# Six weight loads cut into a transfer of 40 rows and one of 24 rows, in a kernel of sparse attention followed by a spectral mix

## The chip, the cores and the metric

The kernel runs on one core of one Trainium2 chip. The metric is the time of one execution on the device in microseconds (us), as the median of several runs. All inputs lie in the chip's memory as 32-bit floats; the kernel turns them into 16-bit floats while it loads them.

## The reference

The first half is causal attention with 8 batches, 8 heads, 576 positions and 64 columns per head. Heads 0 to 3 see the last 32 positions, heads 4 to 7 see every 32nd position. The second half takes the result as x (8 x 576 x 512), goes to frequencies, mixes the lowest 64 of them with a complex 512 x 512 matrix each, comes back, and ends in a channel product:

```
X = np.fft.rfft(x, axis=1)
Xr, Xi = real and imaginary part of X[:, :64]
Yr = einsum('bmd,mde->bme', Xr, w_r) - einsum('bmd,mde->bme', Xi, w_i)
Yi = einsum('bmd,mde->bme', Xr, w_i) + einsum('bmd,mde->bme', Xi, w_r)
y = np.fft.irfft(Y, n=576, axis=1)        # Y is zero above mode 63
u = x + y
out = u + max(u @ w_ch, 0)
```

The weights w_r and w_i are 64 matrices each of 512 x 512. They are 134 MB as 32-bit floats, and each is used once.

## The kernel before

The weights are a stream of 128 tiles. Tile i holds, for mode m = i % 64, one half of the 512 input rows (the upper half for i < 64, the lower for i >= 64): 256 rows of w_r in partitions 0 to 63 and the same 256 rows of w_i in partitions 64 to 127, four rows to a partition. The function `w_fetch` makes the next tile and issues its loads on GpSimd's queue: one transfer for w_r and one for w_i, each of 64 partitions by 2048 numbers, which is 256 KB as it lands and twice that as it is read (line 190). Mode 0 has no imaginary part, so tiles 0 and 64 have one transfer. That makes 254 transfers. In what follows a "row" is one partition's 2048 numbers, so a transfer has 64 rows.

The tiles live in a pool of 11 buffers (`NWBUF`), besides six early "guests" in other buffers. Each transfer issued from GpSimd takes one of eight completion semaphores in turn, and the issue waits until the transfer that used that semaphore eight places earlier has landed. A tile's first transfer also waits for TensorE to be done with the buffer. GpSimd's queue carries the loads of q, k and v as well: pieces of 64 rows (line 216), small pieces of 8 rows (line 222) and pieces of 128 shorter rows (line 234).

The work has four stages. The strided heads come first, with loads ahead of them. Then the local heads run, and the first 64 calls of `mode` (slot 0) are spread between their steps. The third stage runs `mode(1, m)` for the other 64 tiles, between the transposes and channel products of `turn` and `premix` (lines 587 to 651). Each `mode` is 16 products of a weight block with the spectra X (line 543) and, at its end, one call of `w_fetch`, so one tile is ordered for one used. The order of the steps on TensorE is the order in which they are written. The fourth stage comes after the last mode: it turns the spectra back, adds, and writes the output, with no weights left to load.

Tiles are numbered by `i`, so the tile used by `mode(slot, m)` is i = 64 * slot + m.

Of the kernel before, what the change touches and what calls it, by code (L numbers as in the profile page):

```python
# [19 lines left out]
NM = 64  # L20
# [59 lines left out]
def kernel(  # L80
# [10 lines left out]
    nc = tc.nc  # L91
# [76 lines left out]

    GUEST = {3: ("Y0", 0), 4: ("Y0", 1), 5: ("X0", 0), 6: ("X0", 1)}
    GUEST |= {15: ("YT", 0), 16: ("YT", 1)}  # L170
    guests = {}
    w_tiles = []
    w_chs = {}

    def w_fetch(n=1):
        for _ in range(n):
            i = len(w_tiles)
            if i >= 2 * NM:
                return
            half, m = 1 - i // NM, i % NM  # L180
            if i in GUEST:
                n, j = GUEST[i]
                if j == 0:
                    guests[n] = big.tile([128, 2, 4, DM], F16, tag=n, name="wt")
                wt = guests[n][:, j]
            else:
                wt = pw.tile([128, 4, DM], F16, tag="w", name="wt")

            for ri, src in enumerate([moe_w_r, moe_w_i] if m else [moe_w_r]):
                nc.gpsimd.dma_start(  # L190
                    wt[ds(64 * ri, 64)],
                    src[m, ds(256 * half, 256), :].rearrange("(p c) e -> p c e", c=4),
                )
            w_tiles.append(wt)

    def w_ch_fetch():
# [335 lines left out]
    def mode(slot, m):  # L532
# [17 lines left out]
        if slot or m not in GUEST:  # L550
            w_fetch()
# [145 lines left out]
    const_load(nc.sync, "cMl", "cFl", "cA")  # L697
    load_str(2)
    w_fetch(2)

    def str_front(b):
# [39 lines left out]
    for b in range(B):  # L741
        if b < 5:
            load_str(b + 3)
        load_loc(*[(), (), (), (), (0,), (1, 2), (3,), (4, 5)][b])
        w_fetch([3, 3, 2, 2, 2, 1, 1, 1][b])
        front = str_front(b + 1) if b + 1 < B else loc_front(0)
        for t in range(6):
            str_scores(b, t)
            if b > 0:
                if t < 2:  # L750
                    str_values(b - 1, 4 + t)
                elif t == 2:
                    dft(b - 1, 1)
            if t >= 2:
                str_values(b, t - 2)
            for w in front[SPLIT[t] : SPLIT[t + 1]]:
                w()
        if b == 1:
            nc.vector.memset(PL[:, 0:PS0], 0.0)
# [241 lines left out]
```

The softmax here doesn't subtract the row's maximum and nothing guards it: scores larger than these inputs give would overflow.

## Time and profile before

| | |
|---|---|
| median of 6 runs | 438.34 us (437.3 to 439.75) |
| profiled execution | 437.52 us, span from first to last instruction 435.7 us |
| busy share of the span | TensorE 77%, VectorE 50%, ScalarE 43%, GpSimd 43% |
| mean granted TensorE clock | 0.838 of full speed |
| bytes moved | 92.20 MB as it lands, 163.22 MB read from memory |
| GpSimd's transfer queue | 26800 packets, 81.29 MB, 94.8% of the 16 transfer engines' time |
| one weight transfer | 256 KB, 9.4 to 9.6 us from issue to landing (median) |

The profile follows one execution. A transfer is done by 16 transfer engines side by side; a full row of 2048 numbers is one packet of 4096 bytes as it lands, and an engine works on one packet after the other. The chain of waits goes back from the last instruction to whatever released it, again and again, and so shows what set the time in each stretch. The profiled execution took 1.82 us more than its span, for what lies before the first and after the last instruction.

### The profile page before, as it was taken

The numbers are of one execution on the slowest core, as the hardware profiler recorded it, in microseconds if no ns is written. First come the engines' busy times: TensorE is split into PE (matmuls) and PEld (weight loads), VectorE is DVE, ScalarE is ACT, GpSimd is POOL, SyncE is SP. The second block draws the span as 40 slices with busy tenths as digits, with TensorE's granted clock in tenths as the row PEclk, the third lists the DMA queues.
The fourth block names the chain that finished last, engine by engine and source line by source line (L and its number), as shares of the span: only waits on it lengthen the run. The fifth ranks groups of instructions, "written<-read, shape, count | busy, mean of one in ns | idle before, by whom it ended". The sixth has DMA issues, their size and how long they took to land.

```text
span 435.7 us, 12328 instructions
## 1 busy us (share of the span) xinstructions
PE 334.8 (77%) x5289; PEld 241.4 (55%) x5289; DVE 215.9 (50%) x466; ACT 188.4 (43%) x353; POOL 186.7 (43%) x339
## 2 busy tenths in 40 slices
PE   1988778779897878787775566778685858988994
PEld 1866667558776666576653344445444545554441
DVE  2786887935335243343411033344344443764895
ACT  1585777744554345434441201123222312443882
POOL 6545353333444343444343444344344344420883
PEclk9996999979888678967865559686978688999999
DMA  8999999999999999999999999999999999991687
GB/s 172 207 211 211 211 212 212 211 209 212 213 210 213 211 208 211 212 212 212 212 209 214 211 211 212 212 212 213 199 212 212 212 211 213 211 211 36 266 323 281
DMA packets 31094, 92.20 MB, mean 212 GB/s; under 512 B 6144, under 2 KB 7168, under 8 KB 31040
## 3 DMA queue, kind: packets, MB, share of 16 engines
q0 software_dynamic: 26800, 81.29, 94.8%
q1 hardware_dynamic: 3440, 9.46, 5.8%
q8 instruction: 42, 0.69, 0.6%
q10 hardware_dynamic: 800, 0.67, 0.6%
q14 instruction: 12, 0.10, 0.1%
HBM read 163.22 MB, written 9.44 MB: 396 GB/s over the span
## 4 chain that ended last, share of the span: by engine, by line
DMA 75%; PE 15%; issue 4%; DVE 3%; ACT 1%; POOL 1%; DVEq 0%; POOLq 0%
DMA wt<-in_moe_w_i_dram 56%; DMA wt<-in_moe_w_r_dram 11%; DMA ring<-in_q_dram 6%; PE sc L641 2%; DMA ring<-in_v_dram 2%; PE u L684 2%; PE v L684 2%; PE v L886 2%; PE y L543 1%; DVE yy L674 1%; PE u L905 1%; PE tp L281 1%; PE tp L320 1%; PE tp L649 1%; DVE xT L593 1%
## 5 line engine op out<-in xcount | busy, mean ns | idle before, releaser
L543 PE MATMUL y<-X,wt 128*128 128x16 f16 (+1 forms) x2048 | 82.6, 192 | 60.7 <-DMA wt<-in_moe_w_i_dram 58.4
L190 POOL DMA_DIRECT2D wt<-in_moe_w_r_dram x128 | 65.8, 514 | 120.0 <-DMA wt<-in_moe_w_r_dram 34.2
L543 PEld LDWEIGHTS <-wt 128*128 128x128 f16 (+1 forms) x2048 | 72.2, 103 | 75.1 <-issue 54.1
L190 POOL DMA_DIRECT2D wt<-in_moe_w_i_dram x126 | 64.8, 514 | 67.1 <-DMA wt<-in_moe_w_i_dram 49.3
L650 ACT ACTIVATE v<-sc 128x512 f16<-128x512 f32 x32 | 19.0, 597 | 86.0 <-PE sc L641 85.9
L641 PE MATMUL sc<-w_cp,xT 128*128 128x512 f16 (+1 forms) x160 | 49.1, 434 | 0.5 <-DVE xT L613 0.4
L467 ACT ACTIVATE PL<-sc 128x480 f16<-128x480 f32 (+1 forms) x48 | 27.7, 579 | 46.2 <-PE sc L453 45.7
L651 DVE COPY xo<-tp 128x512 f16<-128x512 f16 x32 | 22.1, 692 | 41.9 <-PE tp L649 41.9
L246 DVE TENSOR_TENSOR xb<-av,rec 90x256 f16<-90x256 f32 (+2 forms) x80 | 36.0, 450 | 2.8
L245 DVE RECIPROCAL rec<-av 90x4 f32<-90x4 f32 (+2 forms) x80 | 14.7, 183 | 42.8 <-PE av L482 30.4
L398 DVE COPY qT<-tp 128x576 f16<-128x576 f16 x16 | 12.0, 758 | 41.2 <-PE tp L391 38.3
L256 ACT ACTIVATE v<-tp 128x640 f16<-128x640 f16 (+1 forms) x24 | 19.4, 807 | 20.3 <-PE tp L425 16.7
L391 PE MATMUL tp<-cI_s,ring 64*64 64x64 f16 x864 | 26.4, 212 | 1.9 <-DVE kz L398 1.2
L356 ACT ACTIVATE PL<-sc 90x360 f16<-90x360 f32 (+1 forms) x48 | 22.9, 490 | 10.7 <-PE sc L349 10.0
L899 POOL TENSOR_TENSOR rl<-rl,xo 128x512 f32<-128x512 f32 x16 | 18.3, 1156 | 18.2 <-ACT rl L897 17.9
L916 DVE TENSOR_TENSOR osb<-u,rl 128x512 f32<-128x512 f32 x36 | 23.6, 689 | 2.6 <-PE u L684 1.5
L391 PEld LDWEIGHTS <-ring 64*64 64x64 f16 x864 | 21.0, 124 | 6.6 <-issue 3.6
L437 PE MATMUL sc<-cMl_s,cI_s 128*128 128x480 f16 (+1 forms) x48 | 22.6, 471 | 1.6 <-ACT X L256 1.6
L453 PE MATMUL sc<-qT,kz 128*128 128x160 f16 (+1 forms) x160 | 22.6, 267 | 1.3 <-issue 1.3
L281 PE MATMUL tp<-cI_s,ring 72*128 72x72 f16 x256 | 15.2, 207 | 10.4 <-DMA ring<-in_v_dram 7.8
L453 PEld LDWEIGHTS <-kz 128*128 128x128 f16 x160 | 16.3, 117 | 11.6 <-issue 8.9
L897 ACT ACTIVATE rl<-v 128x512 f32<-128x512 f32 x36 | 20.4, 597 | 4.2 <-PE v L684 3.5
(98 smaller groups left out, 641.0 us busy)
## 6 DMA issues: line engine op xcount, KB each, us to landing
wt<-in_moe_w_r_dram POOLq DMA_DIRECT2D x128, 256.0 KB, 9.4
wt<-in_moe_w_i_dram POOLq DMA_DIRECT2D x126, 256.0 KB, 9.6
out_dram<-osb SPq DMA_DIRECT2D x14, 512.0 KB, 2.7
ring<-in_v_dram POOLq DMA_DIRECT2D x8, 288.0 KB, 10.2
ring<-in_q_dram POOLq DMA_DIRECT2D x8, 288.0 KB, 10.6
ring<-in_k_dram POOLq DMA_DIRECT2D x8, 288.0 KB, 10.6
ring<-in_v_dram POOLq DMA_DIRECT2D x8, 256.0 KB, 8.5
ring<-in_q_dram POOLq DMA_DIRECT2D x8, 256.0 KB, 8.4
```

What stands on the lines that cost most here:

```text
L190: nc.gpsimd.dma_start(wt[ds(64 * ri, 64)], src[m, ds(256 * half, 256), :].rearrange("(p c) e -> p c e", c=4),)
L246: nc.vector.tensor_tensor(out=dst, in0=val.rearrange("p h (q c) -> p h c q", c=4), in1=rec[0:n, 0:pieces] .to_broadcast((n, pieces, 64)) . ...
L356: nc.scalar.activation(out=PS[0:n, ds(POFF[t], 4 * n)], in_=scp[0:n, 0 : 4 * n], func=ACTF.Exp, scale=SCALE,)
L391: nc.tensor.transpose(tp[ds(64 * hp, 64), ds(64 * i, 64)], qn[ds(64 * hp, 64), ds(64 * (9 * g + i), 64)], idn[ds(64 * hp, 64), ds(64 * hp, ...
L437: nc.tensor.matmul(scp[:, 0 : n * times].rearrange("p (h x) -> p h x", h=times), idn, mask_rows("cMl", n, times), start=True, stop=False,)
L453: nc.tensor.matmul(scp[:, ds(col, n)], kzs[par][:, hp, ds(s0, 128)], qTs[par][:, ds(s0, n)], start=False, stop=(i == len(todo) - 1),)
L467: nc.scalar.activation(out=dst, in_=src, func=ACTF.Exp, scale=SCALE)
L543: nc.tensor.matmul(yv[:, mi, e, :], wt[pr, XC[c], ds(128 * e, 128)], Xh[half][pr, c, :, :, m], start=(c == 0), stop=(c == 3),)
L641: nc.tensor.matmul(vp[pr, :], xT[:, ch, cols], w_chs["cp"][:, ch, :], start=(ch == 0), stop=(ch == 3),)
L651: nc.vector.tensor_copy(out=xo[pr].rearrange("p (h q c) -> p h q c", h=2, c=4), in_=tp[pr, 0:512].rearrange("p (h c q) -> p h q c", h=2, c=4),
L897: nc.scalar.activation(out=rl, in_=vp, func=ACTF.Relu)
L916: nc.vector.tensor_tensor(out=osb[:, t % 2, :], in0=up, in1=rls[b, t][:, t % 2, :], op=AluOp.add)
```

## The change

In six of the 128 tiles (i = 28, 45, 62, 79, 96 and 113) the load of the w_r part is issued as two transfers, one of the first 40 rows and one of the remaining 24, in place of one of 64 rows. The same bytes go to the same places. The w_i parts and the other tiles are loaded as before.

```
     GUEST |= {15: ("YT", 0), 16: ("YT", 1)}
+    CUT = range(28, 2 * NM, 17)
...
             for ri, src in enumerate([moe_w_r, moe_w_i] if m else [moe_w_r]):
-                nc.gpsimd.dma_start(
-                    wt[ds(64 * ri, 64)],
-                    src[m, ds(256 * half, 256), :].rearrange("(p c) e -> p c e", c=4),
-                )
+                rows = src[m, ds(256 * half, 256), :].rearrange("(p c) e -> p c e", c=4)
+                cuts = (0, 40, 64) if i in CUT and not ri else (0, 64)
+                for a, z in zip(cuts, cuts[1:]):
+                    nc.gpsimd.dma_start(wt[64 * ri + a : 64 * ri + z], rows[a:z])
             w_tiles.append(wt)
```

GpSimd's queue has 336 rows of program in place of 330; the other engines have the same number of instructions in the same order. The first product of a cut tile waits for three semaphores in place of two, and the transfers behind a cut use the next semaphore in the circle of eight.

## The prediction

> **What bounds the kernel now.** I read the page's strip of slices first, then the chain of waits, then who waits for the weights.
>
> ```profile
> PE   1988778779897878787775566778685858988994
> DMA  8999999999999999999999999999999999991687
> ...
> q0 software_dynamic: 26800, 81.29, 94.8%
> ...
> L543 PE MATMUL y<-X,wt 128*128 128x16 f16 (+1 forms) x2048 | 82.6, 192 | 60.7 <-DMA wt<-in_moe_w_i_dram 58.4
> ```
>
> The transfer engines are full from the first slices to slice 36 (about 392 us), and TensorE's idle time before the mode products is put down to the w_i transfer, 58.4 of 60.7 us. So the stream of weights sets the pace. The chain says how evenly:
>
> ```profile
> 317.41 9.63 DMA wt<-in_moe_w_i_dram
> 327.04 0.28 issue
> 327.32 9.63 DMA wt<-in_moe_w_i_dram
> 336.95 0.28 issue
> 337.23 9.63 DMA wt<-in_moe_w_i_dram
> ...
> 366.82 0.65 PE y L543 x16
> ```
>
> Each link is a transfer, then the issue of the transfer eight places behind it, which had to wait for its semaphore. So eight transfers take 9.63 + 0.28 = 9.91 us, one takes 1.239 us. With 64 rows on 16 engines, an engine does four packets in that time: about 0.305 us each and 0.02 us for its completion mark.
>
> A transfer has landed when its slowest engine has. The trace holds 16 landing marks for each transfer; no view prints them, so I give them in numbers. For the weight transfer that lands at 137 us the first and the last mark are 3.0 us apart, for one at 253 us 4.3 us, for the last weight transfer (396.56 us) 4.2 us. Then eight engines lie within 0.4 us of the first, and the other eight between 3.4 and 4.2 us behind it. The cause stands in the queue list:
>
> ```profile
> q8 instruction: 42, 0.69, 0.6%
> ```
>
> These are 42 blocks of program of 16 KB, 0.9 to 1.3 us each. Their durations recur in a cycle of eight (893, 893, 948, 945, 936, 974, 974, 962 ns), and at each one landing mark steps back by about 1.07 us. So eight engines take turns at them, about five each by the end, and the stream runs at the pace of these eight. None of the 16 stands idle: each shows 1.239 us for every weight transfer.
>
> Last, how the stream hands over to the end. In the stretch from 340 to 400 us TensorE waited for weights only this long, and the last tile is used 1.0 us after it landed:
>
> ```profile
> PE y L543 <- DMA wt<-in_moe_w_i_dram: 5.6, 5, 1.5
> ```
> ```profile
> 395.73 0.64 PE L543 MATMUL y<-X,wt 128*128 128x16 f16 x16
> 397.08 1.12 PE L543 MATMUL y<-X,wt 128*128 128x16 f16 x32 [0.72 <-DVE YT L571]
> ```
>
> Setting each tile's landing against its use: tiles 109 to 115 are used 0.05 to 0.3 us after they land, tiles 116 to 119 0.25 to 0.7 us after, tile 125 4.2 us after. So from about 367 us the chain is TensorE's and VectorE's own work, started by tile 115. A delay of the stream before that reaches the end less about 0.25 us of slack (tile 118); a gain reaches it only as far as TensorE can follow.
>
> **The change part by part.** *Issues.* Six transfers more on GpSimd's queue. The form with 8 rows, the nearest to a small one, takes 0.57 us to issue, the 64-row form 0.51 us:
>
> ```profile
> L222 POOL DMA_DIRECT2D ring<-in_q_dram x4: 573/573/591, 3.0 to 51.9; - x4
> ```
> ```profile
> L190 POOL DMA_DIRECT2D wt<-in_moe_w_r_dram x128: 509/515/554, 14.4 to 385.9; - x128
> ```
>
> Six times 0.57 us is 3.4 us, beside a queue that stands waiting for landings (97 us in all). Behind the added issue on that queue are the tile's w_i load and the following tiles; they wait for a landing anyway. Price: nothing. Without that cover it would be up to 3.4 us.
>
> *Semaphores.* Two small transfers hold two of the eight places, so the queue holds up to one transfer (1.24 us) less. From issue to the first landing mark a late weight transfer takes 5.0 to 5.4 us, against 4.1 us for the kernel's very first transfer, which found the engines empty. So about 1 us of work lies queued before the leading engine, and some 5 us before a lagging one. With 1.24 us less, a leader may stand idle for a moment at a cut, a laggard never does, and only the laggards set the pace. Price: nothing; without that cover up to 0.3 us a cut, 1.5 us in all.
>
> *Completion marks.* What an engine without data pays shows in the 8-row pieces of line 222. Their packets go to eight engines only, two each (0.63 us), and the other eight spend 0.04 us on marks. One more transfer is thus 0.02 to 0.04 us per cut and engine: 0.12 to 0.24 us for six, on every engine. I take 0.24.
>
> *The split of the rows.* This is the term that decides. 64 rows are four for each of 16 engines; 40 and 24 rows are not multiples of 16, so some engines get more than four of the tile's rows and some fewer. No weight transfer before shows how. The nearest row is the 8-row piece: twelve of them, one set of eight engines and the other in turn. Three bounds follow.
> - Same engines each time: five rows in place of four on most engines, laggards among them, six times: 6 x 0.305 = +1.83 us. With the marks, +2.07 us.
> - Shares move on from cut to cut: what is left over is at most about one piece, 0.63 - 0.04 = 0.59 us, on a few engines. With the marks, +0.24 to +0.83 us.
> - All eight laggards are spared a row each time: -1.83 + 0.24 = -1.59 us, and the leaders, at 0.4 + 2.07 = 2.5 us, stay ahead of the laggards' 4.2 - 1.6 = 2.6 us.
>
> Would dealing 40 rows to one set of eight (five each) and 24 to the other (three each) spare the laggards? I followed the marks through the pieces between 27 and 62 us. The engines that never fetch program come from both sets, so laggards sit in both, and the set with five rows would hold some: again +1.83 us. I therefore take the first bound as the likeliest.
>
> A rule that bears on this stands in the Trainium skill, DMA: Bandwidth & Descriptors, section on why a DMA increments its semaphore by 16: the number of engines is the largest one up to 16 that divides the row count, and fewer than 16 start where the last such transfer ended. By it, 40 rows are ten engines with four and 24 rows twelve with two; over six cuts four engines end two rows up, four two rows down, and the estimate from that page is between -0.4 and +0.8 us. The same section reports an exception for transfers from GpSimd: all 16, with the rounded-up share each. By that, 40 rows are three each and 24 two each, so the first twelve engines do five rows each time, an estimate of +1.9 us. The alternating 8-row pieces agree with the rule's start that moves on; no run here shows which of the two holds for 40 rows. The page's rules for kernel authors also advise against two transfers to disjoint partition halves, since the parts share the same engines.
>
> *Sum.* The stream's slowest engine is 2.07 us later by tile 113; less 0.25 us of slack is 1.8 us. The last laggards differ by 0.8 us among themselves, so the worst need not be hit fully: I take 1.7 us. The profiled 437.52 us become 439.2. That execution lies 0.82 us under the median, so on the scale of medians: 438.34 + 1.7 = 440.0 us. What this kernel's measurement can tell from no change is about 0.3%, or 1.3 us.
>
> **The rivals.** *The shares even out* (0.29). For it: the 8-row pieces do move on. Against it: a start that moves is seen only for transfers on half the engines. +0.24 to +0.83 us in the stream, less 0.25: 0 to 0.6 us, so 438.3 to 438.9 us. No change that can be told.
>
> *The laggards are spared* (0.15), the other side. If the rows dealt less fall on the eight engines that fetch the program, the slowest engine gains up to 1.59 us. For it: six cuts of one row either way are 3.7 us between two sets of eight, and the gap to close is 3.4 to 4.2 us. Against it: both sets of the 8-row pieces hold laggards. TensorE must follow: in the slack table tile 105 is used 4.1 us after it lands, and it has caught up by 109, so it can follow most of it. About -1.3 us: 437.0 us. It decides from about three rows of relief on each of the eight; with fewer the worst of them stays.
>
> *The cut does nothing because the loads are the same bytes* would be the first rival with no marks: 438.3 us; it is in its chance.
>
> **How the numbers follow.** Uneven shares on fixed engines has 0.56, and its own range is 439.3 (the worst laggards hit in part, +1.0) to 440.9 us (+2.07, no slack, and half a us of scatter; the runs before spread from 437.3 to 439.75). The range for 8 in 10 takes in the first rival and goes from 437.9 to 441.0 us. Of the forecast some falls under 0.3%, of the first rival some above, and these are about equal: faster 0.15, same 0.29, slower 0.56.
>
> **What would show it.** Right: in the chain, links of 9.63 us as before except around the six cuts, where a link grows by about 0.3 us; the last weight transfer lands about 2 us later than 396.56; the 16 marks of the late transfers lie further apart than 4.2 us; TensorE's wait for weights grows. The even rival would show the same last landing within 0.8 us, the other one a last landing near 395 us and marks closer together. Wrong altogether would be a stream in which engines stand idle at the cuts (a queue run dry), or a chain that no longer goes through the weights before 366 us.

## The result and the profile after

The change costs time: 440.80 us as the median (439.77 to 442.31), against 438.59 us for the kernel before beside it. The ratio is 1.0051, with a 95% interval from 1.0040 to 1.0061, so +2.2 us (1.8 to 2.7). All changes of the time in us below are worked out from such ratios; the medians alone give up to 0.6 us more or less. The profiled execution took 440.23 us with a span of 438.3 us; before they were 437.52 and 435.7 us. The forecast was 440.0 us, about 1.7 us slower; of the 0.8 us between it and 440.80 us, 0.25 us is the median of the kernel before, which was 438.34 us when the forecast was made. All lines of the kernel after stand three or more higher: the weight load is L196, the mode products L546.

The strips and the two rows of the page that answer to those of before:

```profile
PE   1977787779795988878854567678585859988994
DMA  8999999999999999999999999999999999991687
...
q0 software_dynamic: 26992, 81.29, 94.8%
...
L546 PE MATMUL y<-X,wt 128*128 128x16 f16 (+1 forms) x2048 | 82.1, 192 | 62.3 <-DMA wt<-in_moe_w_i_dram 60.0
```

The transfer engines are as full as before, with the same 81.29 MB, and TensorE waits 1.6 us longer for the same 2048 products (60.7 us before). That wait is a poor measure, though: in the kernel with 25 such cuts, some 10 us slower (below), it is 59.6 us. The queue has 192 packets more. What they are, the experiments show.

The chain of waits in the stretch of the cut in tile 79:

```profile
258.06 9.63 DMA wt<-in_moe_w_i_dram
267.69 0.28 issue
267.97 9.05 DMA wt<-in_moe_w_r_dram
...
278.19 9.76 DMA wt<-in_moe_w_i_dram
287.95 0.28 issue
288.24 9.63 DMA wt<-in_moe_w_i_dram
```

Away from the cuts the links are still 9.63 + 0.28 us. At a cut, two of the eight transfers in flight are small ones, and the chain changes from w_i transfers to a w_r transfer and back, so one link is shorter and the next a little longer. The chain therefore doesn't show the price of a cut; the landing marks do. The last weight transfer landed at 398.90 us, 2.34 us later than before. Of these, 0.25 us were there at tile 24 already, ahead of the first cut; that is scatter between two executions.

The page's summary of the chain changed far more than the time did, first before and then after:

```profile
DMA 75%; PE 15%; issue 4%; DVE 3%; ACT 1%; POOL 1%; DVEq 0%; POOLq 0%
```
```profile
DMA 50%; PE 31%; DVE 11%; issue 3%; ACT 3%; POOL 1%; DVEq 0%; POOLq 0%
```

These shares don't price the change either. A kernel with 25 even cuts and two additions moved, which is as fast as the one before (below), shows 48% DMA. In the kernel after, the chain runs through TensorE's own work from 341.5 to 350.5 us, where a transfer was issued only once TensorE was done, and goes back to the weights until 368.9 us.

How the stream hands over to the end, first the wait between 340 and 400 us, then the last products on TensorE's timeline:

```profile
PE y L546 <- DMA wt<-in_moe_w_i_dram: 6.8, 6, 1.6
```
```profile
397.89 0.59 PE L546 MATMUL y<-X,wt 128*128 128x16 f16 x16
399.20 1.12 PE L546 MATMUL y<-X,wt 128*128 128x16 f16 x32 [0.72 <-DVE YT L574]
```

The last two groups start at 397.89 and 399.20 us, in place of 395.73 and 397.08 us. The use of the last tile (the second half of the last group of 32) moved from 397.56 to 399.67 us, +2.11 us: the 2.34 us less 0.23 us of slack. But the span grew by 2.6 us. The other 0.5 us came after the last tile was used, where no weight is left to load. The prediction had nothing there.

### The profile page after: what moved, and what is told of

Read it like the earlier page. It is cut to its first block, busy times and chain, and to the rows that moved or that the text cites. A ratio compares the mean times of both kernels' runs of the same rounds, so it can differ in the third digit from the quotient of the medians.

```text
span 438.3 us, 12336 instructions
## 1 busy us (share of the span) xinstructions
PE 334.9 (76%) x5289; PEld 240.9 (55%) x5289; DVE 216.1 (49%) x466; ACT 188.5 (43%) x353; POOL 190.6 (43%) x345
## 3 DMA queue, kind: packets, MB, share of 16 engines
q0 software_dynamic: 26992, 81.29, 94.8%
## 4 chain that ended last, share of the span: by engine, by line
DMA 50%; PE 31%; DVE 11%; issue 3%; ACT 3%; POOL 1%; DVEq 0%; POOLq 0%
DMA wt<-in_moe_w_i_dram 37%; DMA wt<-in_moe_w_r_dram 11%; PE y L546 5%; PE sc L644 4%; DVE kz L291 3%; DVE xb L249 2%; PE tp L394 2%; PE u L687 2%; PE v L687 2%; PE v L889 2%; DMA ring<-in_q_dram 2%; PE sc L513 2%; PE sc L440 1%; ACT X L259 1%; PE sc L456 1%
## 5 line engine op out<-in xcount | busy, mean ns | idle before, releaser
L546 PE MATMUL y<-X,wt 128*128 128x16 f16 (+1 forms) x2048 | 82.1, 192 | 62.3 <-DMA wt<-in_moe_w_i_dram 60.0
L196 POOL DMA_DIRECT2D wt<-in_moe_w_r_dram x134 | 69.3, 517 | 122.3 <-DMA wt<-in_moe_w_r_dram 28.2
L546 PEld LDWEIGHTS <-wt 128*128 128x128 f16 (+1 forms) x2048 | 72.1, 103 | 76.2 <-issue 65.5
L196 POOL DMA_DIRECT2D wt<-in_moe_w_i_dram x126 | 65.2, 517 | 63.0 <-DMA wt<-in_moe_w_i_dram 38.5
L644 PE MATMUL sc<-w_cp,xT 128*128 128x512 f16 (+1 forms) x160 | 51.4, 451 | 0.5 <-DVE xT L616 0.4
L644 PEld LDWEIGHTS <-xT 128*128 128x128 f16 (+1 forms) x160 | 14.8, 111 | 15.0 <-issue 7.3
```

The source lines that it names most:

```text
L196: nc.gpsimd.dma_start(wt[64 * ri + a : 64 * ri + z], rows[a:z])
L546: nc.tensor.matmul(yv[:, mi, e, :], wt[pr, XC[c], ds(128 * e, 128)], Xh[half][pr, c, :, :, m], start=(c == 0), stop=(c == 3),)
L644: nc.tensor.matmul(vp[pr, :], xT[:, ch, cols], w_chs["cp"][:, ch, :], start=(ch == 0), stop=(ch == 3),)
```

## The experiments

Nearly all edits are made in two lines, the set of tiles that are cut and the rows of the parts. The kernel after has

```
CUT = range(28, 2 * NM, 17)                                    # six tiles
cuts = (0, 40, 64) if i in CUT and not ri else (0, 64)
```

**Six cuts of 32 and 32 rows.**

```
-cuts = (0, 40, 64) if ...
+cuts = (0, 32, 64) if ...
```

> The same six tiles, the w_r part cut as 32 and 32 rows, so that each transfer is a multiple of 16 rows. Theory (the cost is the deal of the rows: 40 rows go three to an engine and 24 rows two to an engine, always from the same first engine, so twelve engines get five of 64 rows): here each engine gets two and two, and only 6 more completion marks of 0.02 us are left, 0.13 us; the time is that of the kernel before, within 0.4 us. Rival (the cost is in the six transfers more: their issue, the semaphore places they hold, the marks): about the same 2.2 us over the kernel before as the changed kernel. Second rival (the start of an uneven share moves on): also within 0.4 us.

Measured: 438.34 us, ratio 1.0017 (1.0007 to 1.0027), +0.7 us. The last landing is 0.49 us later than before, but 0.38 us of that were there at tile 24; the cuts themselves made 0.1 us. So with even rows the stream hardly notices six cuts, and most of the 2 us is the uneven rows. The time is a little over the expected bound; the reason is found at the end of the kernel, below. In this kernel's profiled execution another thing shows: its span is 438.2 us, as long as that of the kernel after. TensorE's clock was at half speed for 3.41 us at 388.5 us. The stretch from 388 to 392 us, in this kernel and then in the kernel before (columns: stretch, length, busy time and instructions of PE, PEld, DVE, ACT and POOL, granted clock, share of the transfer engines, which can read a little over 1, and GB/s):

```profile
388.00:392.00 4.00, 4.00 (x32) 2.33 (x33) 0.72 (x2) 0.96 (x2) 0.00 (x0) 0.57 1.07 214
```
```profile
388.00:392.00 4.00, 4.00 (x57) 2.64 (x55) 2.07 (x3) 1.79 (x3) 0.00 (x0) 1.00 1.05 212
```

TensorE was busy throughout and got 32 matmuls done in place of 57. The use of the last tile came 2.02 us later than before and the last landing only 0.49 us, so the stretch cost about 1.5 us; from tile 115 on the chain is TensorE's own work. Between 367 us and the last few us, no such stretch begins in the traces of the kernel before and of the kernel after; one does in those of six other kernels here.

**Twenty-five cuts of 40 and 24 rows.**

```
-CUT = range(28, 2 * NM, 17)
+CUT = range(28, 2 * NM, 4)
```

> 40 and 24 rows in every fourth tile from 28 on: 25 cuts in place of six. Theory (fixed first engine): twelve engines do 0.305 + 0.02 us more per cut, 25 cuts make 8.1 us, less up to 1 us for the last cuts, which come after the end has stopped following the stream: 7.1 to 8.1 us over the kernel before, about 446.2 us. Rival (the shares even out from cut to cut): 25 cuts leave the marks, 25 x 0.04 = 1.0 us, and at most a piece of 0.6 us: 1 to 1.6 us over the kernel before, about 440 us.

Measured: 447.40 us, ratio 1.0229 (1.0215 to 1.0244), +10.0 us. The last landing is 7.94 us later, 0.14 us of it ahead of the cuts: 7.80 / 25 = 0.31 us a cut, one row's 0.305 us. Shares that even out are ruled out. Yet the time is some 2 us above what the theory expected. The use of the last tile moved by 7.24 us and the span by 9.29 us, so here 2.05 us came after the weights, against 0.5 us with six cuts.

**Six cuts into 20, 20 and 24 rows.**

```
-cuts = (0, 40, 64) if ...
+cuts = (0, 20, 40, 64) if ...
```

> The same six tiles, the w_r part cut as 20, 20 and 24 rows. Theory (rows dealt two to an engine each time, from the same first engine): ten engines get six of 64 rows, two more than before; with two more marks of 0.02 us this is 0.65 us per cut, 3.9 us in all, and the time is 3.6 to 4.2 us over the kernel before. Rival (as many engines as divide the row count, each share starting where the last one ended: ten, ten and twelve engines with two rows each are 32 shares of two rows, which is four rows on every engine): only the marks, 0.2 to 0.5 us over the kernel before.

Measured: 443.67 us, ratio 1.0144 (1.0125 to 1.0163), +6.3 us. The landing is 5.18 us later, 4.39 us more than at tile 24: 0.73 us a cut, in place of two rows' 0.61 us and marks. That fits shares that are rounded up for each part by itself, with the excess on the same engines. After the use of the last tile the span grew by 0.98 us. That term was missing in the expectation again. Even with it the sum is 4.39 - 0.23 + 0.98 = 5.1 us, under the interval of the time (5.5 to 7.1 us); the rest stays unexplained.

**Eight cuts with a first part of 8, 4, 12, 6, 2, 10, 14 and 8 rows** (tiles 26, 37, 48, 66, 77, 88, 99, 110).

```
+CUT = {26: 8, 37: 4, 48: 12, 66: 6, 77: 2, 88: 10, 99: 14, 110: 8}
+cuts = (0, CUT[i], 64) if i in CUT and not ri else (0, 64)
```

> One look, to see in the landing marks how a small first piece is dealt and which engines lag: eight tiles (26, 37, 48, 66, 77, 88, 99, 110) are cut into a first piece of 8, 4, 12, 6, 2, 10, 14 and 8 rows and the rest. Theory: a piece of n rows goes one row each to the first n engines, always the same ones, and the rest (50 to 62 rows) four to an engine from the same first engine, so the first n engines step back by 0.3 us against the middle ones and the last engines gain about 1.2 us. By the tiles it touches each engine has its own row of steps, from which its place in the order can be read. The time should be 1.8 to 2.7 us over the kernel before if an engine among the first two is a laggard (eight cuts of 0.33 us), less if the laggards are further on. Rival (small pieces start where the last one ended): steps fall on other engines at each cut, and the time is within 1 us of the kernel before.

A single run, so its time says little: 438.97 us; last landing 0.71 us later (0.32 us at tile 24). That is far less than eight rows, so a small part does not hit the slowest engines each time. Which engines it hits can't be read: the marks carry no engine's name, and more than one assignment fits them. What this run gives is the count of packets, used next.

**What the packet count says.** A transfer of 64 rows makes 64 packets and 16 marks. These are the queue rows of the kernels with 6 even cuts, 25 even cuts (told below), 25 uneven cuts, 20, 20 and 24 rows, and eight small parts; before it was 26800:

```profile
q0 software_dynamic: 26896, 81.29, 94.2%
```
```profile
q0 software_dynamic: 27200, 81.29, 94.2%
```
```profile
q0 software_dynamic: 27600, 81.29, 93.9%
```
```profile
q0 software_dynamic: 27184, 81.29, 93.9%
```
```profile
q0 software_dynamic: 27056, 81.29, 94.5%
```

An even cut adds 96 / 6 = 400 / 25 = 16 packets, the marks of one more transfer. A cut into 40 and 24 adds 800 / 25 = 192 / 6 = 32. The 16 more are what is missing to the next multiples of 16: 40 + 8 = 48 and 24 + 8 = 32. The other cuts fit to the packet. 20, 20 and 24 lack 12 + 12 + 8 = 32, and the queue shows 64 a cut with 32 marks; each of the eight cuts with a small part lacks 16 in all, and the queue shows 32 a cut. The sizes in the trace say what the added packets are. The 4096-byte packets are 17984 in every kernel here; all that is added is packets of 4 bytes, the size of a mark. So the parts of a cut are dealt to all 16 engines with the rounded-up share, and who has no row left gets a filler of 4 bytes. The 8-row pieces of line 222 fit as well: the kernel before has 5232 packets of 4 bytes, 16 marks for each of its 315 transfers and 16 fillers for each of the twelve pieces; the prediction had read them as a deal to eight engines alone. Which engine a share starts with no count shows. 40 rows are three for each engine until they run out, 24 rows are two; if both begin with the same engine, twelve engines have five rows of the tile, one has three, one has one and two have none. The marks at the first cut of the kernel after (tile 28), which carry no engine's name, fit that: against the pace of 1.239 us a transfer most of the 16 moved back by 0.31 to 0.36 us, and a few moved ahead, one that had been last by 0.9 us.

**Twenty-five cuts of 32 and 32 rows, and the same with GpSimd's last two additions moved.** Where did the time after the last tile come from? The profile's views used here don't name it, since they show no drain of GpSimd. (A drain is the closing instruction that each engine has at the kernel's end, before it signals the others.) The trace holds them. GpSimd's last instruction before the common end is a drain that starts at about the same time as its last addition (L899 before) and ends 6.05 us after that addition's end. Before the change it ended at 434.95 us, 0.22 us after SyncE's drain, which waits for the last output. In the kernels so far it takes, from the end of the last addition:

| transfers on GpSimd's queue | kernel | drain's end after the last addition | span's end after the use of the last tile |
|---|---|---|---|
| 315 | before | 6.05 us | 38.18 us |
| 321 | after, and six even cuts | 6.54 us | 38.67 and 38.66 us |
| 323 | eight small parts | 6.71 us | 38.83 us |
| 327 | 20, 20 and 24 | 7.03 us | 39.16 us |
| 340 | 25 uneven cuts | 8.09 us | 40.22 us |

Both columns grow by 0.082 us a transfer, whatever its rows. From the use of the last tile to the end of the last addition it is 31.33 to 31.34 us in all of them, so the growth is the drain's. Two runs put that to the test: as many transfers as in the kernel with 25 uneven cuts, first with even rows, then with an earlier start of the drain. `pool_adds` names the rows whose addition of x GpSimd does; the others go through TensorE.

```
-CUT = range(28, 2 * NM, 17)
+CUT = range(28, 2 * NM, 4)
-cuts = (0, 40, 64) if ...
+cuts = (0, 32, 64) if ...
```

> Twenty-five tiles are cut, each 32 and 32 rows: as many transfers as in the kernel with 25 cuts of 40 and 24 rows, but four rows of each tile for every engine. Theory (the uneven rows cost about 0.3 us a cut; each added transfer costs 0.02 to 0.04 us of marks in the stream, and 0.08 us at the end, where GpSimd's last drain grows with the transfers that its queue has issued): stream 0.5 to 1.0 us later, last landing about 397.1 to 397.6 us, GpSimd's last drain ends 8.09 us after its last add (6.05 us before the change), together +2.3 to +3.0 us. Rival (any cut costs 0.3 us, whatever its rows): +7 to +10 us, as with 40 and 24. Rival (transfers are free, only rows cost): within 0.7 us of the kernel before.

```
 # pool_adds, besides the 25 even cuts
-if (b, t) in ((0, 1), (B - 1, 3)):
+if (b, t) in ((0, 1), (B - 1, 1), (B - 1, 3), (B - 1, 4)):
     return False
```

> The same twenty-five even cuts, but the last two of GpSimd's additions (rows 1 and 4 of the last batch) go to TensorE, as those of other rows do, so that GpSimd starts its last drain about 2.6 us earlier. Theory (the drain is what holds the end): the drain takes 8.09 us from the last addition again, but ends before the last output has landed, so 1.5 to 2.0 us less than with the adds left on GpSimd; +0.5 to +1.2 us against the kernel before. Rival (the drain waits for something else that ends late): the drain ends where it did, and the time is the same as with the adds, or longer by TensorE's two more matmuls (about 0.5 us).

Measured with the adds on GpSimd: 440.27 us, ratio 1.0048 (1.0028 to 1.0068), +2.1 us; with the adds moved: 438.09 us, ratio 0.9993 (0.9978 to 1.0008), -0.3 us. The landing of the first is 1.40 us later (0.43 at tile 24), of the second 0.56 us (0.01), so 0.02 to 0.04 us a cut. So leaving the adds on GpSimd costs 2.2 us by the medians, a little more than the 1.5 to 2.0 us expected; both times came out lower than I had expected, the second by 0.8 us. Against 25 uneven cuts, with the same number of transfers, the even rows with the adds on GpSimd save 7.9 us (10.0 less 2.1). Of the last landing even rows save 6.8 to 7.2 us, or 0.27 to 0.29 us a cut: nearly a row. And the end belongs to the drain: both kernels' drains end 8.09 us after the last addition, but 2.29 us after SyncE's drain in the first (438.36 and 436.07 us) and 0.33 us before it in the second (434.84 and 435.17 us). The last stretch of the kernel before, of the kernel with 25 even cuts and then with the adds moved; the columns are those of the stretches above:

```profile
434.60:435.70 1.10, 0.00 (x0) 0.00 (x0) 0.00 (x0) 0.00 (x0) 0.00 (x0) 0.50 0.00 0
```
```profile
436.00:439.20 3.20, 0.00 (x0) 0.00 (x0) 0.00 (x0) 0.00 (x0) 0.00 (x0) 0.50 0.00 0
```
```profile
435.00:435.90 0.90, 0.00 (x0) 0.00 (x0) 0.00 (x0) 0.00 (x0) 0.00 (x0) 0.50 0.00 0
```

With 25 even cuts, no engine computes and no byte moves for the last 3.2 us. The view has no name for it, but a stretch of nothing at the end is how it looks. With the adds moved 0.9 us are left; from the last drain to the span's end every kernel here takes 0.77 to 0.80 us.

**Six cuts of 47 and 17 rows.**

```
-cuts = (0, 40, 64) if ...
+cuts = (0, 47, 64) if ...
```

> The same six tiles, cut 47 and 17. Theory (each transfer of 16 rows or more is dealt the rounded-up share from the same first engine): 47 rows are three for engines 0 to 14 and two for engine 15, 17 rows are two for engines 0 to 7 and one for engine 8; so engines 0 to 7 do five rows, engine 8 four, engines 9 to 14 three. If the eight engines that fetch program are engines 7 to 14, as the marks of the runs so far suggest, only engine 7 of them is hit: the last mark of the last weight transfer is 1.2 to 2.0 us late, alone, and six laggards' marks are 1.8 us earlier than its own would have been, so a gap of 1.5 us or more opens before the last mark. Time +1.5 to +2.3 us with 0.5 us of the longer drain. Rival (shares move on): marks as before, time +0.5 to +1.0 us.

Measured: 440.19 us, ratio 1.0039 (1.0021 to 1.0057), +1.7 us; last landing 1.57 us later (0.44 at tile 24), and 192 packets more, as 1 + 15 missing rows a cut make it. At the cut in tile 113 the marks, measured against the pace of 1.239 us a transfer from some fixed zero, were, before it, 6.83, 7.61, 9.30 and 9.55 us for the last four, and after it 6.55, 7.30, 9.62 and 9.89 us on the same scale. So the last two moved back by 0.33 us, a row and a mark, while the next two moved ahead by 0.3 us. The gap before the last ones is 2.3 us. The deal fits again. My guess which engines are the slowest does not: two of those that fetch program, not one, have five rows.

**An attempt at a faster kernel: 48, 7, 7 and 2 rows, with the adds moved.**

```
-cuts = (0, 40, 64) if ...
+cuts = (0, 48, 55, 62, 64) if ...      # and pool_adds as above
```

> An attempt at a faster kernel: the same six tiles, cut 48, 7, 7 and 2 rows, with GpSimd's last two additions on TensorE. Theory A (small transfers too start at the same first engine): engines 0 and 1 do six rows, 2 to 6 five, 7 to 15 three; if the laggards are engines 7 to 14 they gain 0.305 us a cut less three marks of 0.02 to 0.04: 1.1 to 1.5 us by the end, last landing near 395.3 us; the 18 more transfers lengthen GpSimd's drain by 1.5 us, which the earlier start hides. Time -1.0 to -1.5 us, at most. Theory B (transfers of fewer than 16 rows start where the last one ended, as the 8-row loads of the input do): the three small ones cover the 16 engines once, four rows for each: stream +0.4 to +0.7 us, time +0.2 to +0.7 us. Rival (small transfers empty the queue of eight): a stall of up to 1 us a cut, +2 to +6 us.

Measured: 439.78 us, ratio 1.0027 (1.0011 to 1.0042), +1.2 us, between the second theory and the rival. The drain was hidden (the span ends 37.77 us after the use of the last tile), so all of it is the stream. The last landing is 3.08 us later, and the 16 marks of the last transfer lie 2.41 us apart in place of 4.2. They came closer because the leaders lost their lead: within three transfers after the cut in tile 113 the first mark fell back by 1.5 us against the pace of 1.239 us a transfer. I read this as the leading engines running out of work, with three of the eight places taken by parts of at most 7 rows; no run tests that reading. Where the small parts begin was not settled.

**The change with the adds moved, and the kernel before with the adds moved.**

```
-if (b, t) in ((0, 1), (B - 1, 3)):
+if (b, t) in ((0, 1), (B - 1, 1), (B - 1, 3), (B - 1, 4)):
```

> The change as it is, with GpSimd's last two additions on TensorE. Theory (of the +2.2 us, 0.5 us is GpSimd's longer last drain, and the rest the stream): the drain ends before the last output has landed, the last weight landing stays about 398.9 us; 0.5 to 0.8 us less than the change without this, +1.4 to +1.8 us against the kernel before. Rival (all of the 2.2 us is the stream): +2.0 to +2.6 us.

> The kernel before, no tile cut, with GpSimd's last two additions on TensorE. Theory: GpSimd's drain, 6.05 us from its last addition, ends about 2.4 us before the last output has landed, in place of 0.2 us after it: -0.2 to -0.3 us, which the times alone can hardly tell, and the span then ends with SyncE's drain. Rival (TensorE's two more matmuls lie on the chain of the last rows): +0.3 to +0.6 us.

Measured: 440.18 us, ratio 1.0045 (1.0029 to 1.0061), +2.0 us for the first; 437.78 us, ratio 0.9996 (0.9979 to 1.0013), for the second. The times can't tell either from the kernel it was made from: the intervals are 1.4 to 1.5 us wide. The first was expected at +1.4 to +1.8 us, and +2.0 us is where its rival's range begins, so for six cuts the time alone does not show the drain's part. The profiles do. In the first the drain ends at 437.31 us, 1.81 us before SyncE's, and the span ends 37.86 us after the use of the last tile, 0.81 us less than in the kernel after. That is more than the 0.49 us by which the drain grew: in the kernel after SyncE's drain, too, came late, 37.57 us after the use of the last tile in place of 37.17 us before and 37.09 us here. (Its last tile was used late, at 402.03 us, with a stretch of half clock at 390 us; its last landing, at 398.83 us, is that of the kernel after.) In the second the drain ends 3.2 us before SyncE's, but a half-clock stretch at 397 us hides what that was worth. So the step is right and too small to be measured as time, and no version here beats the kernel before by an amount that can be told.

**Six cuts of 40 and 24 rows, all early, and all late.**

```
-CUT = range(28, 2 * NM, 17)
+CUT = range(28, 70, 8)          # early; late: range(117, 128, 2)
```

> The same 40 and 24 rows in six tiles, all early (28, 36, 44, 52, 60, 68). Theory (the slowest engines set the pace from the first tile on, so where a cut lies before tile 115 makes no difference): the last landing 2.0 to 2.4 us later, the landings of tiles 80 to 127 all late by the same 2 us, time +2.0 to +2.6 us. Rival (an early delay is made up from the lead of the other engines or from loads that wait for buffers): the difference shrinks after tile 68, time +0.5 to +1.2 us.

> The same 40 and 24 rows in six tiles, all late (117, 119, 121, 123, 125, 127). Theory (each cut delays the stream by 0.33 us, and from tile 116 on TensorE uses a tile 0.25 to 4.2 us after it has landed, tile 127 1.0 us after): last landing +2.0 us, use of tile 127 about +1.1 us, with 0.5 us of the longer drain +1.4 to +1.7 us. Rival (no slack that counts, each delay is passed on): +2.2 to +2.6 us. Rival (the end is TensorE's own, the stream doesn't matter there): +0.5 us, the drain alone.

Early: 440.88 us, ratio 1.0060 (1.0038 to 1.0082), +2.6 us; last landing 1.94 us later. The end is as expected: six early cuts cost as much as six spread ones. In between it is not: the landings are 1.8 us late at tile 80, 1.0 us at tiles 92 to 109 and 2.3 us at tile 112. The kernel after dips at tile 92 too, to 0.5 us. The marks and the queue `q8 instruction` show what moves there. In the kernel before, the last mark steps back by 1.0 us against the pace at tile 91, with a block of program fetched at 304.9 us; in the kernel after and in the early one the blocks fetched at 304.2 and 304.6 us move the last mark by 0.3 us at most, so the difference shrinks. In the early kernel the last mark steps back by 1.3 us at tile 112, with the block fetched at 359.0 us, and the difference returns. So a landing in the middle of the stream carries up to about 1 us for which engine fetched program last; the last landings agree better, 1.9 to 2.1 us for six cuts from tile 24 on, in four kernels.

Late: 440.30 us, ratio 1.0050 (1.0033 to 1.0067), +2.2 us, with an interval from 1.4 to 2.9 us that holds both the theory's and the first rival's time. The trace tells them apart. The last landing is 1.91 us later and the use of the last tile 0.96 us, so the slack of the last tiles took about half. The landings fall behind cut by cut: by nothing at tile 118, 0.34 us at tile 120, 0.94 us at tile 122, 1.85 us at tile 124, 1.56 us at tile 126, 1.91 us at tile 127. (This span is 2.9 us longer than before: 0.96 us, 0.49 us of drain and, by what is left, 1.48 us of a half-clock stretch at 400 us.) Why the median is higher than 0.96 + 0.49 us would give is not settled.

## Why the prediction was right, and where it was not

**The split of the rows** was the term that decides, and its size held. I took the bound "same engines each time", five rows in place of four, 0.305 us and 0.04 us of marks a cut. A cut into 40 and 24 moved the last landing by 0.35 us in the kernel after, 0.31 us with 25 cuts and 0.33 us with six late ones. My reason for it was partly luck. I argued with two sets of eight, five rows for the one and three for the other; by the packets and marks twelve engines got five rows. And some laggards seem to have been spared: in the last transfer of the kernel after only five marks stand within 0.5 us of the last, where before all eight slow engines stood within 0.8 us. Five that are hit are enough to move the last mark the full way. The rival of shares that move on fails at 25 cuts (last landing 7.9 us later), and the rival of spared laggards fails with it: sparing some of the eight gains nothing. Of the two statements in the Trainium skill, DMA: Bandwidth & Descriptors, section on why a DMA increments its semaphore by 16, the exception is what happened: all 16 engines, with the rounded-up share (its estimate was +1.9 us in the stream, the cuts made 2.1 us). The rule of the largest divisor with a start that moves describes none of the uneven cuts tried here; packet counts and, for parts of 16 rows or more, marks speak against it.

**The marks** were sized right: 0.02 to 0.04 us a cut in the runs with even rows. **The semaphores** at nothing held for one extra transfer a tile, as the same runs show, and seems to have failed for three, where the marks look as if the leaders ran dry.

**The issues** at nothing is the step that was mis-sized. Their cover, a queue that waits, is real while the stream runs: 25 more transfers with even rows cost the stream 0.6 to 1.0 us, all of it of the size of marks. But each issued transfer also lengthens GpSimd's last drain by 0.082 us. In the kernel before, that drain already ended 0.22 us after the last output, so six transfers cost 6 x 0.082 = 0.49 us with no cover. In time this is shown with 25 cuts, where moving the additions gave back 2.2 us; with six it is shown in the traces only. I looked at the queue where it waits and not at what it does at the end.

**The sum.** By the runs: six rows and their marks about 2.0 us, less 0.23 us of slack (I had 0.25), and 0.49 us of drain make 2.3 us; measured 2.2 us. The 0.1 us taken off because the slowest engines might not all be hit was not needed: several runs show the full row. The forecast of 1.7 us was low by 0.5 us, about the missing drain.

**What would show it.** The last landing 2 us later: yes. TensorE's longer wait: yes, by 1.6 us, but with 25 cuts it was 1.1 us shorter than before, so it was no sign to rely on. The marks of the late transfers further apart than 4.2 us: no, they are 4.15 us apart. I had let the engines with fewer rows run ahead, but the first mark of the last transfer moved back by 2.40 us, as far as the last one. I read this as the limit of eight transfers in flight: engines that are ahead run out of work and wait, and the spread stays. Links longer by 0.3 us at the cuts: not readable, since the chain changes its transfer there. The chain left the weights for 9 us at 341.5 us, but went back to them before it passed to TensorE for good at 368.9 us, so the sign for wrong altogether did not show.

## What to carry to other kernels

In this kernel, transfers of 16 rows or more whose rows are not a multiple of 16 cost the rounded-up share, on engines that did not change from cut to cut; with the transfer engines as the bound, a cut into 40 and 24 rows cost one row. The queue's packet count shows it (more packets than rows and marks). Count also what a transfer costs the engine that issues it at the kernel's end, and start that engine's closing drain early by giving its last work to another. A stretch at the end in which nothing is busy and nothing moves can be a wait that the chain of waits does not name.

## What the hardware showed that I had not expected

GpSimd's last drain took 6.05 us after its last addition with 315 transfers issued and 8.09 us with 340, on a straight line of 0.082 us each through six counts (7.52 us with the 333 of the faster attempt), independent of their rows. What it works off is not known, and the line can't go on far below 315: it would be at zero near 241 transfers. Uneven transfers are filled up with packets of 4 bytes to a multiple of 16. TensorE's clock went to half in stretches of 3.41 us or multiples of it (the last one, at the kernel's end, aside); one that fell between 367 us and the last outputs cost some 1.5 us or more, as much as most effects studied here. The six profiled executions that have one took 0.15 to 2.0 us more than their kernel's median, the others with more than one run between 1.1 us less and 0.7 us more, so it may well be a large part of the 2 us by which executions of one kernel differ.
